# Attention with routed experts: x kept by rows in memory, leftover tokens fetched by an indirect read

## The chip, the cores and the metric

One core of one Trainium2 chip runs the whole program. The metric is device time of one execution in microseconds; the median of several runs counts. Engines: PE (TensorE, matmuls), DVE (VectorE), ACT (ScalarE), POOL (GpSimd), SP (SyncE, which here issues DMAs). Each works through its own instructions in order and waits for the others by semaphores.

## The reference

Attention over keys and values that are averaged in groups of 8 tokens, then a mixture of experts in which every token goes to the best expert (4) of its best group (4):

```
k_p, v_p = mean of k, v over groups of 8 tokens        # 8 batches, 8 heads, 576 tokens, 64
attn = softmax(q @ k_p.T / 8) @ v_p
x = attn.transpose(0, 2, 1, 3).reshape(4608, 512)
g_idx = argmax(x @ w_group); g_w = softmax of it at g_idx
e_idx = argmax(xg @ w_expert[g]); e_w = softmax of it at e_idx
out[token] = g_w * e_w * (relu(x @ w1[g, e]) @ w2[g, e])   # w1 512x1024, w2 1024x512, float32
```

## The kernel before

A batch is 576 tokens, in two halves of 288 (256 and 320 in batch 0). Attention of batch b+1 (class Att) is worked in between the pieces of the experts of batch b (class Moe). x stands transposed: features on partitions, 4 groups of 128, tokens along the free axis. For accuracy x and the weights are each split into a high part that PE reads fast and the low rest: x in tiles `xa`, `xb` (a half each, index 0 high, 1 low; from batch 3 on the unsplit x is in `xr`, L414), the weights by ACT's `cast` (L579, high) and `lo` (L585, `raw - high`, on POOL or DVE). `split` is the two together.

Almost all tokens of a batch want one and the same expert, the main one, which the kernel finds at run time. Moe does the whole batch with it: 16 `up` pieces (8 slices f of the hidden layer, two halves; 12 matmuls each, L602), after each of which ACT (L604) and `upd` on DVE (L610, L615) empty the PSUM tile `mm`, of which there are three; and 14 `down` pieces of 8 matmuls (L631, L642; in the last batch three of 16, L663), after which ACT scales and stores the rows (L636, L668, L683). A chunk of 64 rows is summed by DVE first (L675, `tail`); in batches 2 to 6 that happens one batch later, between the first `up` and its `upd`. The gate is zero for tokens of other experts.

Those are the leftovers. `count` (L483 to L485) counts a batch's tokens by expert; `keep_x` compares (L548 to L552), SP reads the answer, and writes the split x of the batch to memory (`xscr`, two DMAs, L555) only where there are leftovers. With these inputs batch 5 alone has some. In the last batch (class Left, `l.`) the generator `place` (`l.step`, L733 to L768) ranks all leftovers: two matmuls on `loh` with copies L734, masks L738 and L739, a scan and its like to L756, `pos`. `which` (L778 to L785) picks a batch and expert for a block of up to 32 tokens, `slots` (L793 to L810) makes a 128x32 one-hot matrix for each chunk of its tokens, `rows` (L816) turns these into row numbers. `fetch_x` (L834) reads that batch's x back, `whole` (L848) adds its parts, `turn` (L858, 20 PE transposes; copies L859) puts tokens on partitions, `gather` (L866, 40 matmul rows) picks the 32 wanted. `back` (L872), `up` (L880), `hback` (L887) and `down` (L896) work them through their expert, whose weights come by `fetch_a` (L838) and `fetch_b` (L843), and an indirect DMA of POOL scatters them into the output (L899). The later `fetch` calls and a loop at the end are for further blocks, of which there are none here.

What sets the order: the strings START, FIRST (batch 0), SECOND (1), STEADY (2 to 6) and LAST (7). Each name in them is a call, and every engine gets its instructions in the order of the calls: `m.` is the batch's experts, `a.`, `n.`, `x.`, `z.` the attention of this batch, of the next, and of those two and three further on, `w.` the next batch's experts, `p.` the previous one's. In attention, `sc` is scores, `mx`, `su_`, `nm` the softmax (L348, L368 to L370, L375), `pt` its transposition by DVE (L382), `av` the value product (L396), `avd` the emptying of its PSUM (L412, L414), `rt` the routing matmul (L425, L429), `xlo` the low part of x on POOL.

Of the kernel before, what the change touches and what calls it, by code (L numbers as in the profile page):

```python
# [47 lines left out]
m.down:0 w.load:1:2 m.down:1 w.load:1:3 n.sc:1 n.qb:2 n.mx:1 n.pt:0 n.sb:1 m.down:2 m.store:0 n.su_:1 n.nm:1:p x.load_v x.load_k m.down:3 w.split:1:0:p:2 m.down:4 n.sc:2 n.mx:2 n.pt:1 n.sb:2 w.split:1:1:p:2
# [952 lines left out]
```

## Time and profile before

| | us |
|---|---|
| median of 3 runs | 512.82 (512.74 to 513.46) |
| the profiled execution's own time | 513.9 |
| its span, first to last instruction | 512.2 |
| PE busy | 499.5 (98%) |
| DVE busy | 342.1 (67%) |
| POOL busy | 281.5 (55%) |
| ACT busy | 206.3 (40%) |

The granted TensorE clock was 0.995 of full. Busy time is the sum over an engine's instructions; the chain of work is followed back from the last instruction to what released each step. "Idle before, releaser" is how long an engine stood still ahead of an instruction and what ended that. A row of the timeline with xN is a run of N like instructions; the ends of PE rows are modelled and overlap the next row.

### The profile page before, as it was taken

The page shows a single profiled execution, that of the slowest core. Times are in us where ns is not written, and L with a number is a line of the kernel's source. Part 1 is how long each engine was busy: PE and PEld are TensorE (multiplying, and loading weights), DVE is VectorE, ACT ScalarE, POOL GpSimd, SP SyncE. Part 2 cuts the span into 40 slices and gives each one's busy share as a digit, 9 for nine tenths or more (in the row PEclk, how much of TensorE's full clock was granted, in tenths as well). Part 3 has the DMA queues.
Part 4 walks back from the last instruction along what each step waited for, and adds up shares of the span by engine and source line. Part 5 has one row for each costly group of instructions (what it writes and reads, how often), then busy time and mean ns, then how long its engine had stood idle before and what let it go on. Part 6 is the DMA issues. An engine that isn't in the chain of part 4 may idle for free.

```text
span 512.2 us, 14848 instructions
## 1 busy us (share of the span) xinstructions
PE 499.5 (98%) x6085; PEld 439.2 (86%) x6085; DVE 342.1 (67%) x900; ACT 206.3 (40%) x381; POOL 281.5 (55%) x242
## 2 busy tenths in 40 slices
PE   8899999999999999999999999999999999998996
PEld 6688986999789978899789978899789988898976
DVE  6876877678575869486775768476784763199602
ACT  2354324435217541455216551455324551444212
POOL 2386658455818595376728585476846471820400
PEclk9899999999999999999999999999999999999999
DMA  9699279995038976955197616985066100923741
GB/s 281 177 283 192 27 227 228 214 259 89 28 104 233 260 108 177 312 153 83 35 316 207 141 27 143 370 307 88 1 202 184 39 3 22 307 94 124 268 165 58
DMA packets 118110, 83.70 MB, mean 163 GB/s; under 512 B 71034, under 2 KB 93818, under 8 KB 117784
## 3 DMA queue, kind: packets, MB, share of 16 engines
q1 hardware_dynamic: 113408, 75.67, 55.1%
q10 hardware_dynamic: 4600, 7.02, 3.9%
q8 instruction: 49, 0.80, 0.7%
q14 instruction: 21, 0.17, 0.1%
q0 software_dynamic: 32, 0.04, 0.0%
HBM read 77.28 MB, written 28.53 MB: 207 GB/s over the span
## 4 chain that ended last, share of the span: by engine, by line
PE 90%; DVE 4%; DMA 1%; ACT 1%; issue 1%; POOL 1%; POOLq 0%; ACTq 0%
PE mm L602 36%; PE mm L631 30%; PE mm L642 5%; PE sc L336 5%; PE sc L396 4%; PE mm L947 2%; PE tp L429 1%; PE tp L425 1%; DMA out_dram<-y 1%; DMA out_dram<-q,idx 1%; DVE pT L382 1%; POOL p L375 1%; PE tp L299 1%; DVE p L357 1%; PE tp L462 1%
## 5 line engine op out<-in xcount | busy, mean ns | idle before, releaser
L631 PE MATMUL mm<-w,ht 128*128 128x512 f32 x744 | 172.0, 384 | 0.0
L585 POOL TENSOR_TENSOR w<-sw,w 128x1024 fp32r<-128x1024 f32 (+2 forms) x86 | 145.1, 1711 | 40.0 <-ACT w L579 39.9
L631 PEld LDWEIGHTS mm<-w,ht 128*128 128x128 f32 x744 | 137.0, 189 | 25.1 <-issue 6.7
L602 PE MATMUL mm<-xb,w 128*128 128x288 f32 (+1 forms) x768 | 106.7, 291 | 1.7 <-DVE ht L610 1.7
L602 PEld LDWEIGHTS mm<-xb,w 128*128 128x128 f32 x768 | 98.6, 189 | 5.5 <-ACT w L579 2.2
L602 PE MATMUL mm<-xa,w 128*128 128x288 f32 (+1 forms) x768 | 102.3, 286 | 0.5 <-ACT xa L401 0.5
L602 PEld LDWEIGHTS mm<-xa,w 128*128 128x128 f32 x768 | 97.1, 189 | 2.2 <-ACT xa L401 1.0
L604 ACT ACTIVATE ht<-mm 128x288 fp32r<-128x288 f32 (+2 forms) x128 | 52.5, 411 | 94.7 <-PE mm L602 93.0
L375 POOL TENSOR_TENSOR p<-p,su 128x864 f32<-128x864 f32 (+2 forms) x26 | 39.6, 1523 | 76.5 <-DVE su L370 72.0
L579 ACT CAST w<-sw 128x1024 fp32r<-128x1024 f32 x64 | 66.6, 1041 | 31.5 <-DMA sw<-in_moe_w_dram 29.2
L615 DVE SCALAR_TENSOR_TENSOR ht<-mm,ht 128x64 fp32r<-128x64 f32 (+4 forms) x192 | 37.1, 249 | 25.1 <-ACT ht L604 25.0
L636 ACT ACTIVATE y<-mm,gm 128x512 f32<-128x512 f32 x31 | 21.2, 685 | 61.2 <-PE mm L631 61.2
L610 DVE SCALAR_TENSOR_TENSOR ht<-mm,ht 128x288 fp32r<-128x288 f32 (+1 forms) x64 | 27.4, 430 | 13.8 <-ACT ht L604 13.8
L368 DVE TENSOR_REDUCE s<-p 128x12 f32<-128x864 f32 (+2 forms) x26 | 25.4, 976 | 16.5 <-ACT p L362 16.5
L362 ACT ACTIVATE p<-p 128x864 f32<-128x864 f32 (+2 forms) x26 | 22.6, 869 | 28.9 <-DVE p L357 23.6
L382 DVE STREAM_TRANSPOSE pT<-p 128x960 f32<-128x960 f32 (+2 forms) x26 | 28.5, 1095 | 6.7 <-POOL p L375 6.0
L642 PE MATMUL mm<-w,ht 128*128 128x512 f32 x128 | 29.4, 381 | 0.0
L396 PE MATMUL sc<-pT,v 32*64 32x288 f32 (+2 forms) x384 | 27.2, 413 | 1.1 <-DVE pT L382 1.1
L336 PE MATMUL sc<-kT,qT 64*32 64x72 f32 x2176 | 27.9, 230 | 0.2 <-issue 0.2
L336 PEld LDWEIGHTS sc<-kT,qT 64*32 64x32 f32 x2176 | 23.6, 105 | 5.2 <-issue 2.9
L675 DVE TENSOR_TENSOR y<-mm,y 64x512 f32<-64x512 f32 x8 | 5.5, 681 | 32.7 <-ACT y L647 21.7
L396 PE MATMUL tp<-pT,v 32*64 32x288 f32 (+2 forms) x384 | 27.2, 413 | 0.0
(227 smaller groups left out, 565.6 us busy)
## 6 DMA issues: line engine op xcount, KB each, us to landing
sw<-in_moe_w_dram SPq DMA_DIRECT2D x72, 512.0 KB
vv<-in_v_dram SPq DMA_DIRECT2D x27, 320.0 KB
q<-in_q_dram SPq DMA_DIRECT2D x112, 72.0 KB
xscr<-xa SPq DMA_DIRECT2D x7, 1152.0 KB
xscr<-xb SPq DMA_DIRECT2D x7, 1152.0 KB
kv<-in_k_dram SPq DMA_DIRECT2D x14, 512.0 KB
out_dram<-y ACTq DMA_DIRECT2D x23, 256.0 KB
pT<-xscr SPq DMA_DIRECT2D x2, 1152.0 KB
```

The costliest lines, as they stand in the source:

```text
L336: nc.tensor.matmul(ps[x][32 * g:32 * g + 32, SP * t:SP * t + SP], lhsT=s.qT[c][64 * x:64 * x + 64, g, 32 * t:32 * t + 32], rhs=s.kT[64 * x ...
L375: (nc.vector if eng == "v" else nc.gpsimd).tensor_tensor(out=p, in0=p, in1=bc(s.su[c][:, 0:w], SP), op=ALU.mult)
L382: nc.vector.transpose(out=s.pT[:, :, o:o + n].rearrange("p j (t i) -> p t j i", i=32), in_=probs[:, z:z + n // 32].rearrange("p t (j i) -> ...
L396: nc.tensor.matmul(banks[a][64 * x:64 * x + 64, 0:n], lhsT=s.v6[32 * a:32 * a + 32, 5 if x and i == 0 else j, :], rhs=s.pT[32 * a:32 * a + ...
L579: nc.scalar.copy(out=s.w[m, j][0], in_=raw)
L585: (nc.vector if eng == "v" else nc.gpsimd).tensor_tensor(out=wl[:, i:i + n], in0=s.raw[m, j][:, i:i + n], in1=wh[:, i:i + n].bitcast(F32), ...
L602: nc.tensor.matmul(ps[:, 0:n], lhsT=l[:, kc, fs], rhs=apart(s.a.xt[hf][:, r, kc]), start=(kc == 0 and i == 0), stop=(kc == 3 and i == 2))
L604: nc.scalar.activation(out=halves(ht[:, sl]), in_=joined(ps[:, 0:n]), func=AF.Relu)
L610: stt(out=halves(ht[:, 640:640 + n]), in0=ps, scalar=0.0, in1=halves(ht[:, 0:n].bitcast(F32)), op0=ALU.max, op1=ALU.subtract)
L615: stt(out=ht[:, at:at + hi - lo], in0=ps[:, a, lo:hi], scalar=0.0, in1=ht[:, t + lo:t + hi].bitcast(F32), op0=ALU.max, op1=ALU.subtract)
L631: nc.tensor.matmul(ps, lhsT=s.ht[f][:, 640 * l + o:640 * l + o + 128], rhs=apart(s.w[2, f // 2][r][:, f % 2, :]), start=(i == 0), stop=(i ...
L642: nc.tensor.matmul(ps, lhsT=s.ht[f][:, 512:640], rhs=apart(s.w[2, f // 2][r][:, f % 2, :]), start=(i == 0), stop=(i == 15))
```

## The change

x of every batch is kept, unsplit, in memory in row order: one row of 512 for each token (`xrow`). To that end `xr` becomes a tile of 18 blocks of 32 tokens, in each the 4 feature groups side by side, so that DVE can transpose 32x32 squares in place (`xt_`, six instructions of 128x384 for a batch) and four DMAs of SP write it, 288 KB each, without condition (`keep_x`). For batches 0 to 2, whose x was never kept unsplit, ACT writes `xr` from PSUM (`raw`), or POOL adds the two parts (`rawp`, first half of batch 0). Batch 0's `xr` goes out untransposed to `xraw` (`keep_raw`), is read back in batch 5 into the buffer of the values, `vv` (`again`), and is transposed and written by rows in batch 6. The comparison and SP's read of its answer go.

A new plan PENULT serves batch 6: `place` runs there up to the rank, and the first two `lo` of the next weights are on DVE there. In LAST, `which` and `slots` come early, `rows` stands between `up` pieces and gives a third column, the row numbers to read; `get` is an indirect DMA of POOL that reads the 32 wanted pieces straight into `xg`, four partitions of 128 features for each token. `xtiles`, `fetch_x`, `whole`, `turn` and `gather` are gone; `fetch_a` reads its weights with the features in another order, 16 DMAs in place of 4. `l.up` and `l.down` are one `down` piece earlier or more. In FIRST, `count` goes (in SECOND too) and `w.split:1:1` moves behind `n.su_:2 n.nm:2`.

```diff
-m.up:5:0 a.pt:4 n.vr:0 m.upd:5:0 m.up:6:0 m.upd:6:0 m.up:7:0 a.av:1 n.vr:1 n.vm a.rt:0 m.upd:7:0 a.avd:1 n.kr:0
+m.up:5:0 a.pt:4 n.vr:0 m.upd:5:0 m.up:6:0 m.upd:6:0 m.up:7:0 a.av:1 n.vr:1 n.vm a.rawp:0 a.rt:0 m.upd:7:0 a.avd:1 a.raw:1 n.kr:0
...
-m.down:5 m.store:1 m.down:6 n.su_:2 n.nm:2:p m.down:7 n.av:0 n.avd:0 x.load_qb:0 m.down:8 m.store:2 x.vr:0 w.load:2:0 w.load:2:1 n.pt:2 m.down:9 x.kr:0 n.av:1 n.rt:0 n.avd:1 m.down:10 x.kr:1 x.vr:1 x.vm x.load_qb:1 x.load_qb:2 x.load_qb:3 n.rt:1 m.down:11 m.store:3 n.route_g n.route_e:p m.down:12 n.gates n.gm_:p m.down:13 m.store:4
+m.down:5 m.store:1 m.down:6 n.su_:2 n.nm:2:p w.split:1:1:p:2 m.down:7 n.av:0 n.avd:0 n.raw:0 x.load_qb:0 m.down:8 m.store:2 x.vr:0 w.load:2:0 w.load:2:1 n.pt:2 m.down:9 x.kr:0 n.av:1 n.rt:0 n.avd:1 n.raw:1 m.down:10 x.kr:1 x.vr:1 x.vm x.load_qb:1 x.load_qb:2 x.load_qb:3 n.rt:1 m.down:11 m.store:3 n.route_g n.route_e:p m.down:12 n.gates n.gm_:p m.down:13 m.store:4
...
-x.qb:0 n.gates n.gm_ n.xlo:1 n.keep_x m.down:6 x.kt m.down:7 x.sc:0 x.mx:0 x.sd:0 w.cast:1:0 w.lo:1:0 w.load:2:0 m.down:8 x.ex:0 x.qb:1 w.cast:1:1 w.load:2:1 m.down:9
-x.su_:0 x.nm:0:p w.lo:1:1 m.down:10 m.down:11 m.down:12 w.cast:1:2 m.down:13 w.cast:1:3
+x.qb:0 n.gates n.gm_ n.xlo:1 m.down:6 x.kt m.down:7 x.sc:0 x.mx:0 x.sd:0 w.cast:1:0 w.lo:1:0 w.load:2:0 m.down:8 x.ex:0 x.qb:1 w.cast:1:1 w.load:2:1 m.down:9
+x.su_:0 x.nm:0:p w.lo:1:1 n.xt_:0 n.xt_:1 n.xt_:2 m.down:10 m.down:11 n.xt_:3 n.xt_:4 n.xt_:5 n.keep_x m.down:12 w.cast:1:2 m.down:13 w.cast:1:3
...
+PENULT = """
...
+m.up:7:1 m.upd:7:1 n.av:1 n.rt:0 n.avd:1 o.xt_:0 o.xt_:1 o.xt_:2 o.xt_:3 o.xt_:4 o.xt_:5 o.keep_x
+m.down:0 n.rt:1 l.step m.down:1 n.route m.down:2 m.down:3 m.down:4 n.main_expert w.load:1:0 w.load:1:1 w.load:1:2 w.load:1:3 m.down:5
+n.gates n.gm_ n.xlo:1 m.down:6 m.down:7 l.step l.step w.cast:1:0 m.down:8 l.step l.step n.xt_:0 n.xt_:1 n.xt_:2 w.lo:1:0:v w.load:2:0 m.down:9 n.xt_:3 n.xt_:4 n.xt_:5 n.keep_x w.cast:1:1 l.step l.step l.step l.step w.lo:1:1:v w.load:2:1
+m.down:10 l.step l.step l.step m.down:11 l.step l.step l.step l.step l.step m.down:12 m.down:13
...
-l.whole:1 l.turn:1 l.turn:0 l.whole:2 m.lo:2:3:p m.down:2 m.down:3 l.turn:2 m.down:4 l.gather m.down:5 l.back m.down:6 l.up m.down:7 l.hback
-m.down:8 l.down l.fetch_x l.fetch_a l.fetch_b m.down:13 m.down:9 m.down:10 l.slots m.down:11
+m.up:0:0 p.tail m.upd:0:0 l.step m.up:0:1 m.upd:0:1 l.step l.which m.up:1:0 m.upd:1:0 m.up:1:1 m.upd:1:1 l.slots
+m.up:2:0 m.upd:2:0 m.cast:1:2 m.up:2:1 m.lo:1:2:v m.upd:2:1 m.load:2:2 m.up:3:0 m.upd:3:0 m.cast:1:3 m.lo:1:3 m.load:2:3 l.rows l.oh m.up:3:1 m.cast:2:0 m.upd:3:1 l.get m.lo:2:0 l.tiles l.fetch_b:1 m.up:4:0 m.upd:4:0 m.cast:2:1 m.up:4:1 m.upd:4:1 m.lo:2:1
+m.up:5:0 m.upd:5:0 m.up:5:1 m.cast:2:2 m.upd:5:1 m.lo:2:2:v m.up:6:0 m.upd:6:0 m.up:6:1 m.cast:2:3 m.upd:6:1 m.lo:2:3:v l.fetch_a:1 m.up:7:0 m.upd:7:0 l.next_ m.up:7:1 m.upd:7:1
+m.down:0 m.down:1 l.back m.down:12 m.down:2 m.down:3 m.down:4 m.down:5 l.up m.down:6 l.hback m.down:7 l.down
+m.down:8 l.fetch_a l.fetch_b m.down:13 m.down:9 m.down:10 l.slots m.down:11
...
-    xscr = dram.tile([B, 128, 2, 4, S], F32, name="xscr")
+    xraw = dram.tile([128, S // 32, NG, 32], F32, name="xraw")
+    xrow = dram.tile([B * S, DM], F32, name="xrow")
...
-                s.xr = xp.tile([128, NG, S], F32, name="xr")
+                s.xr = xp.tile([128, S // 32, NG, 32], F32, name="xr")
...
+        def rows_(s, h):
+            o, n = s.half[h]
+            return s.rawt()[:, o // 32:(o + n) // 32].rearrange("p j g c -> p g j c")
...
-                    ts(out=s.rawt()[:, g, o:o + n], in0=ps, scalar1=0.125, scalar2=None, op0=ALU.mult)
+                    ts(out=s.rows_(h)[:, g], in0=by32(ps), scalar1=0.125, scalar2=None, op0=ALU.mult)
...
+        def raw(s, h):
+            o, n = s.half[h]
+            for ps, g in s.ta[h]:
+                nc.scalar.mul(out=s.rows_(h)[:, g], in_=by32(ps), mul=0.125)
+        def rawp(s, h):
+            o, n = s.half[h]
+            for g in range(NG):
+                nc.gpsimd.tensor_tensor(out=s.rows_(h)[:, g], in0=by32(s.xt[h][:, 0, g].bitcast(F32)), in1=by32(s.xt[h][:, 1, g].bitcast(F32)), op=ALU.add)
+        def xt_(s, u):
+            z = s.xr[:, 3 * u:3 * u + 3].rearrange("p j g c -> p (j g c)")
+            nc.vector.transpose(out=z, in_=z)
+        def keep_raw(s):
+            nc.sync.dma_start(out=xraw, in_=s.xr)
+        def again(s):
+            s.xr = sk.tile([128, 5, 512], F32, name="vv").rearrange("p a x -> p (a x)")[:, 0:NG * S].rearrange("p (j g c) -> p j g c", g=NG, c=32)
+            nc.sync.dma_start(out=s.xr, in_=xraw)
         def keep_x(s):
-            t = sm.tile([128, NE], F32, name="cr")
-            tt(out=t, in0=s.cnt, in1=s.moh, op=ALU.mult)
-            n = sm.tile([128, 1], F32, name="cm")
-            red(out=n, in_=t, axis=AX.X, op=ALU.add)
-            s.lf = sm.tile([128, 1], I32, name="lf")
-            ts(out=s.lf, in0=n, scalar1=float(S), scalar2=None, op0=ALU.is_lt)
-            left = nc.sync.value_load(s.lf[0:1, 0:1], min_val=0, max_val=1)
-            for h, (o, n) in enumerate(s.half):
-                nc.sync.dma_start(out=xscr[s.b][:, :, :, o:o + n], in_=s.xt[h].bitcast(F32), cond=left, cond_hint=False)
+            to = xrow[S * s.b:S * s.b + S].rearrange("(j i) (a x) -> a i j x", i=32, a=4)
+            for a in range(4):
+                nc.sync.dma_start(out=to[a], in_=s.xr[32 * a:32 * a + 32].rearrange("p j g c -> p j (g c)"))
...
+        def oh(s):
+            ts(out=s.ix, in0=s.mps[:, 2:3], scalar1=s.quarter, scalar2=None, op0=ALU.add)
+            ts(out=s.idx[:, 1:2], in0=s.mps[:, 0:1], scalar1=s.quarter, scalar2=None, op0=ALU.add)
+            nc.vector.tensor_copy(out=s.gl[:, 1:2], in_=s.mps[:, 1:2])
+        def get(s):
+            nc.gpsimd.indirect_dma_start(out=s.xg, out_offset=None, in_=xrow.rearrange("n (d c) -> (n d) c", d=4),
+                                         in_offset=bass.IndirectOffsetOnAxis(ap=s.ix.bitcast(U32), axis=0), bounds_check=4 * B * S - 1, oob_is_err=False)
...
+                for k in range(4):
+                    nc.sync.dma_start(out=s.wa[j][32 * k:32 * k + 32],
+                                      in_=w1x[bass.ds(s.re, 1), k, :, :, 256 * j:256 * j + 256].rearrange("o c a f -> c (o a) f"),
...
-        def whole(s, c):
-            o, n = CH[c]
-            (nc.gpsimd if c % 2 else nc.vector).tensor_tensor(
-                out=s.xh[0][:, :, o:o + n], in0=s.xh[0][:, :, o:o + n], in1=s.xh[1][:, :, o:o + n], op=ALU.add)
...
-                nc.tensor.transpose(out=ps[0:n, 128 * g:128 * g + 128], in_=s.xh[0][:, g, o:o + n], identity=ident)
-            (nc.vector.tensor_copy if c % 2 else nc.scalar.copy)(out=s.xr[0:n, c, :], in_=ps[0:n])
...
-                    nc.tensor.matmul(ps[32 * g:32 * g + BS, 0:128], lhsT=s.sl[c][0:n, 0:BS], rhs=s.xr[0:n, c, 128 * g:128 * g + 128],
-                                     start=(c == 0), stop=(c == NC - 1))
-            nc.scalar.copy(out=s.xg, in_=ps[:, 0:128])
...
-            run(LAST if b == B - 1 else STEADY, b)
+            run(LAST if b == B - 1 else PENULT if b == B - 2 else STEADY, b)
```

On PE, from the end of the last batch's `up` pieces to the end; before (`ident,pT` are the transposes of `turn`, `xb,q` is `gather`):

```order
L816 MATMUL tp<-kT,q 128x2 x5
L858 MATMUL tp<-ident,pT 128x128 x4
L858 MATMUL tp<-ident,pT 64x128 x4
L642 MATMUL mm<-w,ht 128x512 x8
L858 MATMUL tp<-ident,pT 128x128 x8
L631 MATMUL mm<-w,ht 128x512 x16
L858 MATMUL tp<-ident,pT 128x128 x4
L631 MATMUL mm<-w,ht 128x512 x8
L866 MATMUL tp<-xb,q 32x128 x20
L631 MATMUL mm<-w,ht 128x512 x8
```

and of the change, from the first `down` pieces on (L884 is `back`, L892 `l.up`, L908 `l.down`):

```order
L665 MATMUL mm<-w,ht 128x512 x16
L884 MATMUL tp<-ident,q 128x128
L676 MATMUL mm<-w,ht 128x512 x8
L665 MATMUL mm<-w,ht 128x512 x32
L892 MATMUL tp<-sw,q 32x256 x16
L665 MATMUL mm<-w,ht 128x512 x8
L899 MATMUL tp<-ident,q 128x128 x2
L665 MATMUL mm<-w,ht 128x512 x8
L908 MATMUL tp<-kv,q 32x128 x16
L908 MATMUL tp<-vv,q 32x128 x16
```

The transposes and `gather` are gone; the row numbers' matmul (`kT,q`) is not in this piece any more, it stands between `up` pieces.

On DVE at the seam of two batches, before (`y<-mm,y` is L675, the sum of the 64-row chunk):

```order
L368 TENSOR_REDUCE s<-p 128x12
L369 TENSOR_REDUCE su<-s 128x12
L370 RECIPROCAL su<-su 128x12
L675 TENSOR_TENSOR y<-mm,y 64x512
L610 SCALAR_TENSOR_TENSOR ht<-mm,ht 128x288
L382 STREAM_TRANSPOSE pT<-p 128x6x5x32
```

and of the change, the same place:

```order
L381 TENSOR_REDUCE s<-p 128x12
L382 TENSOR_REDUCE su<-s 128x12
L383 RECIPROCAL su<-su 128x12
L576 STREAM_TRANSPOSE xr<-xr 128x384 x6
L709 TENSOR_TENSOR y<-mm,y 64x512
L644 SCALAR_TENSOR_TENSOR ht<-mm,ht 128x288
L395 STREAM_TRANSPOSE pT<-p 128x6x5x32
```

Six transposes of the next batch's x stand between the reciprocal and that sum.

On ACT at the end, before (the activation with `gl` is `l.down`'s, which the scatter of POOL follows; each DMA is a store):

```order
L882 ACTIVATE q<-tp 128x256
L636 ACTIVATE y<-mm,gm 128x512
L683 DMA out_dram<-y 128x512
L898 ACTIVATE q<-tp,gl 128x128
L647 COPY y<-mm 64x512
L676 ACTIVATE y<-y,gm 64x512
L667 ACTIVATE y<-mm,gm 128x256
```

and of the change:

```order
L894 ACTIVATE q<-tp 128x256
L910 ACTIVATE q<-tp,gl 128x128
L670 ACTIVATE y<-mm,gm 128x512
L717 DMA out_dram<-y 128x512
L681 COPY y<-mm 64x512
L710 ACTIVATE y<-y,gm 64x512
L701 ACTIVATE y<-mm,gm 128x256
```

`l.down` now comes ahead of the third chunk's store, which was ahead of it.

## Rows read from the trace of the kernel before

**Rows 1.** page, part 1 (busy us, share, xcount) and part 4 (the chain by engine)
```profile
PE 499.5 (98%) x6085; PEld 439.2 (86%) x6085; DVE 342.1 (67%) x900; ACT 206.3 (40%) x381; POOL 281.5 (55%) x242
...
PE 90%; DVE 4%; DMA 1%; ACT 1%; issue 1%; POOL 1%; POOLq 0%; ACTq 0%
```

**Rows 2.** PE's waits: line <- releaser: us in total, times, longest
```profile
PE mm L602 <- DVE ht L610: 1.7, 1, 1.7
...
PE sc L396 <- DVE pT L382: 1.1, 1, 1.1
```

**Rows 3.** chain that ended last, at the end: start us, us, what
```profile
478.38 1.09 PE tp L858 x8
479.47 1.73 PE mm L642 x8
481.19 0.87 PE tp L858 x8
...
485.52 0.44 PE tp L858 x4
...
487.69 1.36 PE tp L866 x40
...
499.31 2.04 DMA out_dram<-y
...
502.34 3.69 DMA out_dram<-q,idx
...
506.09 1.69 DMA out_dram<-y
```

**Rows 4.** PE in order of time: start, us, line, operation, count
```profile
99.59 0.34 PE L483 MATMUL tp<-oh,ones 128*128 128x80 f32 x2
...
337.24 1.63 PE L602 MATMUL mm<-xa,w 128*128 128x288 f32 x12
...
502.20 5.52 PE L663 MATMUL mm<-w,ht 128*128 128x256 f32 x48
```

**Rows 5.** chain that ended last, late in the first batch (POOL, ahead of L382)
```profile
81.27 1.29 POOL w L585
82.56 1.60 POOL p L375
```

**Rows 6.** DVE in order of time in the last batch, with the idle time before
```profile
448.18 0.68 DVE L675 TENSOR_TENSOR y<-mm,y 64x512 f32<-64x512 f32 x1 [10.98 <-DMA out_dram<-y]
...
449.94 2.69 DVE L585 TENSOR_TENSOR w<-sw,w 128x1024 fp32r<-128x1024 f32 x1
...
465.80 1.22 DVE L585 TENSOR_TENSOR w<-sw,w 128x1024 fp32r<-128x1024 f32 x1
```

**Rows 7.** DVE groups by line and shape: count | busy us, mean ns | idle before
```profile
L382 DVE STREAM_TRANSPOSE pT<-p 128x960 f32<-128x960 f32 x21 | 24.6, 1174 | 5.3 <-POOL p L375 4.5
...
L382 DVE STREAM_TRANSPOSE pT<-p 128x640 f32<-128x640 f32 x4 | 3.3, 827 | 0.6 <-POOL p L375 0.6
...
L734 DVE COPY kv<-tp 128x320 f32<-128x320 f32 x4 | 1.7, 474 | 0.0
...
L738 DVE TENSOR_TENSOR kv<-kv 128x128 f32<-128x128 f32 x4 | 1.1, 283 | 0.0
...
L382 DVE STREAM_TRANSPOSE pT<-p 128x320 f32<-128x320 f32 x1 | 0.5, 512 | 0.8 <-POOL p L375 0.8
```

**Rows 8.** DVE at the seam of batches 4 and 5, in order of time
```profile
330.24 0.23 DVE L370 RECIPROCAL su<-su 128x12 f32<-128x12 f32 x1
333.77 0.68 DVE L675 TENSOR_TENSOR y<-mm,y 64x512 f32<-64x512 f32 x1 [3.30 <-ACT y L647]
```

**Rows 9.** issues on SP's queue in order of time: start, us of issuing, xcount
```profile
324.96 3.94 SPq L555 DMA_DIRECT2D xscr<-xb  x1
329.40 10.23 SPq L573 DMA_DIRECT2D sw<-in_moe_w_dram  x4
...
494.69 1.35 SPq L838 DMA_DIRECT2D sw<-in_moe_w_dram  x4
```

More of the change, by code (lines that the diff above doesn't have):

```diff
@@ L48 @@
[L48 to L49 removed]
+m.lo:2:2:p:2 n.kt m.cast:2:3 m.up:5:1 m.upd:5:1 a.gm_:p a.keep_raw m.lo:2:3:p:2 m.up:6:1 w.load:1:0 w.load:1:1 m.upd:6:1 n.sc:0 n.mx:0 n.sb:0 n.qb:1 m.up:7:1 m.upd:7:1 n.su_:0 n.nm:0:p
@@ L56 @@
-x.sc:0 x.mx:0 x.sb:0 m.down:10 x.qb:1 m.down:11 m.store:3 w.split:1:1:p:2 w.load:2:1 x.su_:0 x.nm:0:p m.down:12 w.cast:1:2 m.down:13 m.store:4
+m.up:0:0 x.load_v x.load_k m.upd:0:0 n.qb:0 m.up:1:0 m.upd:1:0 m.split:1:2:p:2 m.load:2:2 n.kt m.up:0:1 m.upd:0:1 a.xt_:0 a.xt_:1 m.split:1:3:p:2 m.load:2:3 m.up:1:1 m.upd:1:1 a.xt_:2 a.xt_:3 n.sc:0 n.mx:0 m.up:2:0 m.upd:2:0 n.sd:0 n.ex:0 n.qb:1 m.up:2:1 m.upd:2:1 n.su_:0 n.nm:0:p m.split:2:0:p:2
+m.up:3:0 m.upd:3:0 a.xt_:4 a.xt_:5 a.keep_x m.up:3:1 m.upd:3:1 n.sc:1 n.pt:0 n.mx:1 m.up:4:0 m.upd:4:0 n.sd:1 n.ex:1 n.qb:2 m.up:4:1 m.upd:4:1 n.su_:1 n.nm:1:p m.split:2:1:p:2 m.up:5:0 m.upd:5:0 m.split:2:2:p:2 m.up:5:1 m.upd:5:1 n.sc:2 n.mx:2 n.pt:1
@@ new lines @@
+x.load_qb:0 x.load_qb:1 x.load_qb:2 x.load_qb:3 m.up:6:0 m.upd:6:0 n.sd:2 n.ex:2 m.up:7:0 m.upd:7:0 m.up:6:1 n.su_:2 n.nm:2:p m.upd:6:1 m.split:2:3:p:2 m.up:7:1 m.upd:7:1 n.av:0 n.avd:0 n.raw:0 m.down:0 n.pt:2 x.vr:0 m.down:1 x.vr:1 x.vm n.rt:0 m.down:2 m.store:0 n.av:1 n.avd:1 n.raw:1 x.kr:0 m.down:3
+m.down:4 n.rt:1 n.route_g n.route_e:p x.kr:1 m.down:5 m.store:1 m.down:6 x.qb:0 m.down:7 x.kt n.main_expert w.load:1:0 w.load:1:1 w.load:1:2 w.load:1:3 n.gates n.gm_ m.down:8 m.store:2 m.down:9 w.split:1:0:p:2 w.load:2:0
@@ L57 @@
+x.sc:0 x.mx:0 x.sb:0 m.down:10 x.qb:1 m.down:11 m.store:3 w.split:1:1:p:2 w.load:2:1 x.su_:0 x.nm:0:p n.xt_:0 n.xt_:1 n.xt_:2 m.down:12 n.xt_:3 n.xt_:4 n.xt_:5 n.keep_x w.cast:1:2 m.down:13 m.store:4
 """
@@ L70 @@
-m.up:2:0 m.cast:2:1 l.step m.upd:2:0 l.step m.up:2:1 l.step m.upd:2:1 l.step m.up:3:0 l.step l.step m.upd:3:0 m.up:3:1 l.step l.step m.upd:3:1
-m.up:5:0 l.step l.step l.step l.step m.upd:5:0 m.lo:1:3 m.cast:2:2 m.up:4:0 l.step l.step l.which m.lo:2:2:v m.upd:4:0 m.lo:2:1:v
-m.up:6:0 m.cast:2:0 m.upd:6:0 m.up:5:1 m.lo:2:0:v m.up:4:1 m.up:6:1 m.cast:2:3 l.fetch_x l.tiles m.upd:5:1 m.upd:4:1 m.upd:6:1 l.slots m.down:0 m.down:1 l.fetch_a:1
-m.up:7:0 l.fetch_b:1 m.upd:7:0 l.whole:4 l.whole:0 m.up:7:1 l.rows l.next_ l.whole:3 m.upd:7:1 l.turn:3 l.turn:4 m.down:12
@@ L428, in rt @@
             for a in range(4):
[L429 removed]
+                nc.tensor.matmul(ps[32 * a:32 * a + 32, 0:n], lhsT=wr[:, a, :], rhs=s.rows_(h)[:, a], start=True, stop=True)
             nc.scalar.copy(out=lt[:, o:o + n], in_=ps[:, 0:n])
@@ L911, in block @@
             s.rows()
-            for c in range(NC):
-                s.whole(c)
-                s.turn(c)
+            s.oh()
+            s.get()
             s.next_()
-            s.fetch_x()
-            s.gather()
             s.back()
```

70 lines of the change are left out of this document (27 added, 43 removed).

## The prediction

> **What bounds the kernel now.** I read the engine totals first, then the chain of work that ended last, then the list of what TensorE waited for. TensorE (PE) is busy 499.5 of 512.2 us, and 90% of the chain is PE work [rows 1]. So another engine's microsecond is worth something only where PE waits for it, and a PE instruction taken out is worth its own chain time. The list of PE's waits has two that a change of order can remove: 1.7 us in the last batch, where `up` waits for DVE to empty a PSUM tile (L602 for L610), and 1.1 us in the first batch, where the value product L396 waits for DVE's transposed probabilities (L382) [rows 2]. Nothing in the steady batches shows up there at all. The reader is to see that the 90% leaves little for hiding: a gain has to be PE instructions gone or one of these two waits gone, and a loss has to be a new wait of PE or a longer tail after it.
>
> **The change, part by part.** The sum is made against the profiled execution: span 512.2 us, its own time 513.9 us; the median of the runs is 512.82 us, 0.6 above the span. I apply the difference to the median.
>
> *PE work that goes.* The leftover block no longer turns x on PE. The 20 transposes of L858 stand in the chain as 1.09, 0.87 and 0.44 us, together 2.40, and the 40 matmul rows of L866 as 1.36 [rows 3]. All of it is in the last batch with PE as the chain, and nothing replaces it on PE: the 32 wanted rows come by an indirect read. That is -3.76 us. What could take it back is the block's first matmul (L872, `back`) waiting for the read. The nearest row is the indirect scatter, 3.69 us from start to landing [rows 3]; with about 1 us to issue, the read, called after `up` 3:1, has eight `up` pieces (1.63 us of rows each, overlapping a little [rows 4]) and two `down` (1.73 each [rows 3]) before it is used, some 15 us. Hidden. The counts of batches 0 and 1 go too: two matmuls each, 0.34 us of rows that overlap their neighbours [rows 4]; I take half of it for each, -0.3 us together.
>
> *The wait in the first batch.* Before it POOL splits a weight slice (`w.split:1:1`, L585, the last part 1.29 us) and only then normalises p (L375, 1.60), which DVE transposes [rows 5]. The change puts the split behind that normalisation, so p is ready about 1.3 us or more sooner, and the 1.1 us [rows 2] go. What is late next there: the route matmul of the second half, whose PSUM tiles ACT now also reads for `raw` copies; I charge 0.15. Net -0.95 us. Behind the moved split the weights are wanted in the next batch, many us later.
>
> *The wait in the last batch.* Before, DVE there carries the block's bookkeeping. The plan for batch 6 takes the steps up to the rank into a stretch in which DVE idles 10.98 us [rows 6]. Into that hole go: four copies L734 (4 x 0.47 = 1.9), eight mask operations like L738 (8 x 0.28 = 2.2) and eleven more up to L756, of 0.23 to 0.29 us like it (2.7) [rows 7]; the six transposes of batch 7's x; and two weight splits. A split took DVE 1.22 us, and 2.69 in another place [rows 6]. The transposes: 128x320 took 0.512, 128x640 0.827, 128x960 1.174 [rows 7], so a 128x384 is 0.512 + 64 x 0.00098 = 0.575 us by itself, and about 0.5 in a row; six are 3.0 to 3.45. The sum is 6.8 + 3.2 + 2.4 = 12.4, or 15.4 with the dear splits, less 0.5 for the dropped comparison. So the evacuation L675 at the seam starts 1 to 4 us later than at 448.18; it has some 2.8 us before PE wants its tile (below). Then DVE has in the last batch 6.8 us less bookkeeping and three splits where it had four, but the slot masks are wanted already after `up` 3:0, since the row numbers are now matmuls in the middle of the `up` pieces. By laying these in order I get small waits of 0.4 and 0.2 us and then little: 0.9 us of stall in place of 1.67, bounds 0 and 2.5. Net -0.75 us.
>
> By itself, on the splits: at 449.94 the DVE split takes 2.69 us, at 465.80 1.22 [rows 6]. The Trainium skill (GPSIMD Engine Reference, Specifications) says that POOL and VectorE share their SBUF interfaces and contend when DVE has two SBUF inputs, as a split has. By that rule the price depends on what POOL does beside; since batch 6 takes the POOL splits themselves away from that stretch, it speaks for the low price here, and only with other POOL work for 15.4 in place of 12.4, which would make the stall about 2 us.
>
> *What each batch gains to do.* x is kept for all batches, where before the copy is conditional and batch 5 alone was written. Each batch from 1 on gets six in-place transposes on DVE at the seam, ahead of L675, behind the reciprocal. There DVE idles 3.30 us before L675 at 333.77 [rows 8]; six at 0.5 to 0.575 fill that hole to within 0.2 us. L675 ends at 334.45, and the third `up` piece of the batch, which I take for the first to need its tile, starts at 337.24 [rows 4]: 2.8 us more. So they cost nothing; what is queued behind them on DVE (L675, L610, the next L382) moves 0.2 us. I charge 0.3 us over all batches for this and for the strided writes and reads of x in 32-element runs, bounds 0 and 1.5.
>
> *Transfers.* Four unconditional writes of 288 KB per batch, 1.18 MB; batch 0's goes out, comes back and goes out again. On SP's queue they stand before the loads of the next weights (`sw`). The one batch that shows such a write is batch 5, 3.94 us of issuing on SP for the second of its two halves of 1.15 MB, with the loads after it at 329.40 taking 10.23 us to issue [rows 9]; no PE wait comes of it [rows 2]. Half of that batch's bytes in every batch should do no more. The weight fetch of the leftover block is now 16 issues where it was 4; four took 1.35 us [rows 9], so 16 are 5.4 us, ahead of `up` by seven `down` pieces or 12 us. Hidden.
>
> A sentence by itself: the pieces are 512 bytes long, and the Trainium skill (DMA: Bandwidth & Descriptors, Specifications) puts the smallest transfer for full rate at 512 bytes, so by it the writes run at full rate, just; no row of before has this pattern.
>
> *The tail.* Now `down` 8 comes behind the block's last matmul, so its store, on ACT's queue, must wait for the scatter; before it was the other way. With T the end of L896: activation 0.4 and issue 1.0 (before, some 1.0 lies between the landing of the store at 499.31 + 2.04 and the scatter's start) and scatter 3.69 [rows 3] end at T + 5.1; ACT is held at the store until then, and then needs the issue, a copy, L675, an activation and half an activation, about 2.7 us at 0.68 for L675 [rows 8] and like sizes for the rest, so the first half store goes at about T + 7.8 and lands 1.69 to 2.04 later [rows 3], T + 9.5 to 9.9. PE ends after two pieces of 1.73 [rows 3] and the last 5.52 [rows 4], T + 9.0. Before, PE's end (502.20 + 5.52 [rows 4]) and the landing of the first half (506.09 + 1.69 [rows 3]) coincided at 507.7. So the tail grows by 0 to 0.9, more if the scatter is slower; I take 0.4, bounds 0 and 1.5.
>
> **Sum.** -2.40 - 1.36 - 0.3 - 0.95 - 0.75 + 0.3 + 0.4 = -5.06, or 512.82 - 5.1 = 507.7 us.
>
> **Rivals.**
> *DVE too late (B).* The hole takes 15.4 us or the steps wait for each other across PE; then L675 starts past its slack, each `up` tile comes late in turn, and the rows' matmul, which stands between `up` pieces, makes PE wait for slots. Stall 2.5 to 4 us in place of 1.67. For it: PE waits for DVE there already [rows 2], and its order is now tighter. Against: 11 us of hole. It gives 509.3 to 511.
> *Slower (C).* The transposes at the seam cost much more than their row. They work in place on 128x384, and every row of that operation here goes from one buffer to another. The price decides at (3.30 + 2.8) / 6 = 1.02 us each; at 1.17 (the 128x960 row [rows 7]) L675 is late by 0.9 us, and PE with it, in each of six batches, 5.4 us, and the hole of batch 6 overflows by 7 us with two sets of six in or near it, of which some 3 reach PE: +8.4, so 516, with 513 to 518 for prices around it. Against it: the rows of that operation grow evenly with their width.
> *Tail (D).* The scatter's chain is longer by a microsecond than its row, all of which is after PE's end: 508.7 to 510.
> *The change does not do what it says (E).* The writes or the read back hold up weight loads until `up` or `down` waits for a cast, 0.5 to 1 us in each of eight batches: 511.7 to 515.7. Against it stands batch 5.
>
> **How the numbers follow.** The forecast 0.62, with its own range from 506.0 (all stalls gone, no new cost: 512.82 - 2.40 - 1.36 - 1.67 - 1.1 - 0.3) to 509.3; B 0.17; C 0.09; D 0.06; E 0.06. About 0.2%, 1.0 us, is what a measurement of this kernel can tell from no change. Faster than 511.8: the forecast, B and D, less some tails, and a little of E, 0.84; within 0.2%: 0.06; slower: most of C and half of E, 0.10. The range of 8 in 10 goes from 505.5 (a term of the sum too small by half a microsecond) to 512.0 (the lower edge of E); what it leaves out is C, most of E and the edges.
>
> **What would show it.** Right: no PE rows of L858 and L866; neither wait in the list of PE's waits; the transposes at 0.5 to 0.6 us and L675 at the seam of a steady batch moved by less than a microsecond; in the last batch PE waits of under 1 us at `up` or at the rows' matmul; ACT's store of `down` 8 idle until the scatter lands. Wrong: a PE wait on `up` in every batch (C), a cast waiting for `sw` (E), a PE wait of several us between 447 and 470 (B), a last PE instruction well ahead of the last evacuation (D).

## The result and the profile after

The changed kernel takes 506.73 us (median of 4 runs, 506.02 to 507.20) where the kernel before takes 512.78 (4 runs): a ratio of 0.9882 with a 95% interval of 0.9863 to 0.9900, 6.05 us faster. The forecast was 5.06 us faster, 507.7, in a range of 505.5 to 512.0.

The page of the changed kernel: PE's busy time fell by 5.4 us against [rows 1], DVE's rose by 15, and 96% of the chain is now PE.

```profile
PE 494.1 (98%) x6021; PEld 435.9 (86%) x6021; DVE 357.2 (71%) x919; ACT 211.0 (42%) x394; POOL 277.8 (55%) x248
...
PE 96%; DMA 1%; ACT 1%; issue 0%; DVE 0%; SPq 0%; ACTq 0%
```

PE's waits in the changed kernel (line, releaser: us in total, times, longest). Both waits of [rows 2] are gone. Of the waits of half a microsecond and more that are left, all lie in the first 30 us but for the second row, which comes in batch 1 ("issue": the profile shows nothing that PE waited for).

```profile
PE mm L349 <- ACT qT L330: 1.5, 1, 1.5
...
PE sc L349 <- issue: 0.8, 1, 0.8
PE mm L636 <- ACT xa L414: 0.6, 1, 0.6
```

To see where the time went, I cut both spans at three PE rows: the first `up` of batch 1, the first `up` of batch 7, and the end of the last PE row.

| profiled execution, us | to batch 1 | batches 1 to 6 | last batch | after PE's end | span |
|---|---|---|---|---|---|
| before | 96.65 | 350.72 | 60.35 | 4.48 | 512.2 |
| after | 94.35 | 351.70 | 54.01 | 4.94 | 505.0 |
| difference | -2.30 | +0.98 | -6.34 | +0.46 | -7.2 |

The first column's -2.30 holds 1.35 us that the change did not make: PE reached its very first `up`, ahead of all that the change touches on PE, at 26.34 us in place of 27.69, and in after_again, the changed kernel once more, at 27.49 (last section). Without it the spans differ by 5.85 us, close to the medians' 6.05.

The last batch of the changed kernel, PE in order of time (start, us, line, count). There is no idle time in these rows: the 54.01 us are PE's work. The row numbers' matmul (L853) stands between `up` pieces, `back` (L884) follows the first two `down` pieces, and no transposes or `gather` come after it.

```profile
455.07 1.63 PE L636 MATMUL mm<-xa,w 128*128 128x288 f32 x12
456.54 1.26 PE L853 MATMUL tp<-kT,q 128*128 128x3 f32 x10
457.73 1.74 PE L636 MATMUL mm<-xb,w 128*128 128x288 f32 x12
...
471.07 3.62 PE L665 MATMUL mm<-w,ht 128*128 128x512 f32 x16
474.52 0.27 PE L884 MATMUL tp<-ident,q 128*128 128x128 f32 x1
...
494.54 5.52 PE L697 MATMUL mm<-w,ht 128*128 128x256 f32 x48
```

The -6.34 us there are 2.40 and 1.36 of L858 and L866, 1.67 of the wait for DVE, and 0.59 of the ranking's matmuls, which now are in batch 6 (they stand in the +0.98); 0.3 are left over.

DVE in batch 6 of the changed kernel, in order of time: the stretch that held 10.98 us of idle time in [rows 6] is full, with the ranking's copies, six transposes, two weight splits at 1.18 and 1.22 us, and the masks, and L709 (L675 before) ends at 448.81. The third `up`, which needs its tile, begins at 448.99, without a wait, the second of the two PE rows below.

```profile
437.47 0.89 DVE L775 COPY kv<-tp 128x320 f32<-128x320 f32 x2 [1.14 <-PE tp L774]
438.28 1.49 DVE L576 STREAM_TRANSPOSE xr<-xr 128x384 f32<-128x384 f32 x3
439.69 1.18 DVE L619 TENSOR_TENSOR w<-sw,w 128x1024 fp32r<-128x1024 f32 x1
440.79 1.49 DVE L576 STREAM_TRANSPOSE xr<-xr 128x384 f32<-128x384 f32 x3
...
444.16 1.22 DVE L619 TENSOR_TENSOR w<-sw,w 128x1024 fp32r<-128x1024 f32 x1
...
448.13 0.68 DVE L709 TENSOR_TENSOR y<-mm,y 64x512 f32<-64x512 f32 x1
```

```profile
446.05 1.63 PE L636 MATMUL mm<-xa,w 128*128 128x288 f32 x12
...
448.99 1.63 PE L636 MATMUL mm<-xa,w 128*128 128x288 f32 x12
```

DVE at the seam of [rows 8], after: six transposes take 2.81 us, 0.47 each in a row, and the sum still waits 0.89 us for ACT, as it waited 3.30 before.

```profile
328.02 0.23 DVE L383 RECIPROCAL su<-su 128x12 f32<-128x12 f32 x1
328.17 2.81 DVE L576 STREAM_TRANSPOSE xr<-xr 128x384 f32<-128x384 f32 x6
331.87 0.68 DVE L709 TENSOR_TENSOR y<-mm,y 64x512 f32<-64x512 f32 x1 [0.89 <-ACT y L681]
```

### The profile page after: what moved, and what is told of

The parts are those of the page before. It is cut to its first block, busy times and chain, and to the rows that moved or that the text cites. A ratio compares the mean times of both kernels' runs of the same rounds, so it can differ in the third digit from the quotient of the medians.

```text
span 505.0 us, 14775 instructions
## 1 busy us (share of the span) xinstructions
PE 494.1 (98%) x6021; PEld 435.9 (86%) x6021; DVE 357.2 (71%) x919; ACT 211.0 (42%) x394; POOL 277.8 (55%) x248
## 4 chain that ended last, share of the span: by engine, by line
PE 96%; DMA 1%; ACT 1%; issue 0%; DVE 0%; SPq 0%; ACTq 0%
PE mm L636 39%; PE mm L665 33%; PE mm L676 6%; PE sc L349 5%; PE sc L409 4%; PE mm L956 2%; PE tp L447 1%; PE tp L443 1%; PE mm L697 1%; DMA sw<-in_moe_w_dram 1%; PE tp L312 1%; PE tp L409 1%; PE tp L480 1%; PE tp L328 0%; PE tp L908 0%
## 5 line engine op out<-in xcount | busy, mean ns | idle before, releaser
L619 POOL TENSOR_TENSOR w<-sw,w 128x1024 fp32r<-128x1024 f32 (+2 forms) x85 | 142.9, 1704 | 55.9 <-ACT w L613 55.7
L665 PEld LDWEIGHTS mm<-w,ht 128*128 128x128 f32 x744 | 137.1, 189 | 24.9 <-issue 6.1
L361 DVE TENSOR_REDUCE mx<-sc 128x12 f32<-128x864 f32 (+2 forms) x24 | 23.7, 987 | 7.7 <-PE sc L349 7.7
L676 PEld LDWEIGHTS mm<-w,ht 128*128 128x128 f32 x128 | 24.0, 189 | 3.5
## 6 DMA issues: line engine op xcount, KB each, us to landing
sw<-in_moe_w_dram SPq DMA_DIRECT2D x64, 512.0 KB
kv<-in_k_dram SPq DMA_DIRECT2D x14, 512.0 KB
```

What stands on the lines that cost most here:

```text
L619: (nc.vector if eng == "v" else nc.gpsimd).tensor_tensor(out=wl[:, i:i + n], in0=s.raw[m, j][:, i:i + n], in1=wh[:, i:i + n].bitcast(F32), ...
L665: nc.tensor.matmul(ps, lhsT=s.ht[f][:, 640 * l + o:640 * l + o + 128], rhs=apart(s.w[2, f // 2][r][:, f % 2, :]), start=(i == 0), stop=(i ...
L676: nc.tensor.matmul(ps, lhsT=s.ht[f][:, 512:640], rhs=apart(s.w[2, f // 2][r][:, f % 2, :]), start=(i == 0), stop=(i == 15))
```

## Experiments

Eleven kernels were run, each beside the kernel before. Most are the changed kernel with one thing altered. The table cuts their profiled executions as above; "ratio" is to the kernel before, with its interval.

| kernel | median, us | ratio | to batch 1 | batches 1 to 6 | last batch | after PE's end |
|---|---|---|---|---|---|---|
| after_again | 507.17 | 0.9858 (0.9834 to 0.9881) | 95.17 | 351.93 | 54.01 | 4.89 |
| first_old | 507.83 | 0.9880 (0.9857 to 0.9902) | 96.62 | 351.43 | 54.00 | 4.95 |
| tail_old | 507.00 | 0.9864 (0.9842 to 0.9885) | 93.51 | 351.96 | 54.01 | 4.92 |
| read_alone | 512.30 | 0.9966 (0.9949 to 0.9983) | 94.96 | 351.40 | 60.78 | 3.86 |
| read_alone_2 | 508.29 | 0.9929 (0.9901 to 0.9956) | 95.27 | 351.26 | 56.59 | 3.88 |
| write_twice | 512.95 | 0.9994 (0.9978 to 1.0010) | 94.53 | 353.03 | 59.25 | 3.99 |
| write_behind | 518.31 | 1.0100 (1.0068 to 1.0132) | 95.50 | 353.72 | 62.97 | 3.91 |
| write_but_0 | 509.85 | 0.9942 (0.9923 to 0.9960) | 94.56 | 352.94 | 55.02 | 5.68 |
| seam_8 | 507.33 | 0.9893 (0.9879 to 0.9908) | 95.00 | 351.66 | 54.01 | 4.93 |
| seam_12 | 513.11 | 1.0005 (0.9981 to 1.0029) | 95.19 | 357.34 | 54.01 | 4.86 |
| seam_18 | 530.08 | 1.0318 (1.0303 to 1.0333) | 95.06 | 374.38 | 54.00 | 4.96 |

**The yardstick.**

> The changed kernel as it is, as the yardstick for the other runs of this set. Both theories: about 0.988 of the kernel before, some 506.7 us where before is 512.8.

507.17 us. The last batch has 54.01 us again.

**The first batch's order.**

```diff
-... n.pt:1 n.sb:2
-m.down:5 m.store:1 m.down:6 n.su_:2 n.nm:2:p w.split:1:1:p:2 m.down:7 ...
+... n.pt:1 n.sb:2 w.split:1:1:p:2
+m.down:5 m.store:1 m.down:6 n.su_:2 n.nm:2:p m.down:7 ...
```

> The changed kernel with one thing undone: in the first batch the weight split goes back ahead of the normalisation of p. Theory (PE is the chain, and that wait was worth its length less 0.15): 0.95 us slower than the changed kernel, about 507.7, with a wait of PE for the transposed p of about 1.1 us in its list of waits. Rival (the wait is taken up by another one behind it): 506.7, and no change.

PE's wait is back, in the list of waits:

```profile
PE sc L409 <- DVE pT L395: 1.2, 1, 1.2
```

I compare with after_again from the first `up` on (27.67 us here, 27.49 there), since the moved split cannot reach what lies ahead of it. To batch 1 it is 1.27 us longer, and batches 1 to 6 are 0.50 shorter, so 0.77 in the profiles; the medians differ by 0.66, with intervals that overlap. The 0.50 is in one wait of batch 1, in after_again and here:

```profile
PE sc L349 <- issue: 1.1, 1, 1.1
```

```profile
PE sc L349 <- issue: 0.6, 1, 0.6
```

So the theory stands with a size of 0.7 to 0.8 and not 0.95, and the rival is true in part: a wait behind takes up some of what the order gives.

**The indirect read alone.** Is the gain the PE work, or the order?

Batch 6 gets the steady plan without `o.again`, with `o.xt_` and `o.keep_x` behind `n.avd:1`; the last batch gets the plan of before without `xtiles`, `fetch_x`, `whole`, `turn` and `gather`, and with the read (one line of it, against the kernel before):

```diff
-... m.up:7:1 l.rows l.next_ l.whole:3 m.upd:7:1 l.turn:3 l.turn:4 m.down:12
+... m.up:7:1 l.rows l.oh l.get l.next_ m.upd:7:1 m.down:12
```

> The indirect read alone in place of fetch, add, transposes and gather; the ranking steps, the slots and the row numbers stay in the last batch where they were before, and batch 6 has the steady plan plus batch 0's six transposes. Theory: PE's 3.76 us, the first batch's 0.95 and the counts' 0.3 are kept, but PE's wait of 1.7 us for DVE in the last batch comes back: about 508.4. Rival (that wait went because DVE lost the additions and copies of the turn): no wait, 506.7. Rival (what gained was the order, not the PE work): 510 or more.

512.30 us, the third of the expected cases, and at first sight the PE work bought nothing: the last batch takes 60.78 us, before 60.35. PE in order of time shows the wait for DVE as it was, and a second one, for a weight split on POOL:

```profile
466.42 3.24 PE L638 MATMUL mm<-xb,w 128*128 128x288 f32 x24 [1.67 <-DVE ht L646]
...
482.18 8.21 PE L667 MATMUL mm<-w,ht 128*128 128x512 f32 x29 [2.24 <-POOL w L621]
```

POOL in order of time says why. The read (L864) stands ahead of that split in POOL's queue, and POOL stands still for 26.78 us until it can go; the split sits behind it. (The profile names L817, a step of DVE at 478.10; the row numbers `ix`, which the read needs, were written from 477.41 to 477.63.)

```profile
478.51 1.23 POOL L864 DMA_INDIRECT q<-xrow,ix  x1 [26.78 <-DVE kb L817]
479.78 2.35 POOL L621 TENSOR_TENSOR w<-sw,w 128x1024 fp32r<-128x1024 f32 x1
```

After the 2.24 us of waiting PE's granted clock was 0.61 from 482 to 486 (window table: us, busy times of PE, PEld, DVE, ACT and POOL, then clock, DMA share, GB/s), and the stretch cost 4.2 us in all (60.78 less the 56.59 of the next kernel), not 2.24.

```profile
482.00:486.00 4.00, 3.82 (x11) 3.06 (x12) 0.87 (x6) 0.69 (x1) 0.13 (x1) 0.61 0.64 144
```

**The same, with POOL's queue in another order.**

Against read_alone:

```diff
-... m.up:7:1 l.rows l.oh l.get l.next_ m.upd:7:1 m.down:12
-m.lo:2:3:p m.down:2 ...
+... m.up:7:1 m.lo:2:3:p l.rows l.oh l.get l.next_ m.upd:7:1 m.down:12
+m.down:2 ...
```

> As read_alone, but the last weight split on POOL (2:3) stands ahead of the indirect read on POOL's queue, not behind it. In read_alone PE waited 2.24 us for that split, which stood behind the read, and ran at a granted clock of 0.74 in the 6 us around. Theory (queue order on POOL made the new wait): that wait goes and with it about 1.7 us of half clock, so 508.4, with DVE's 1.67 us in the last batch still there. Rival (the read alone gains nothing because PE has nothing to do while weights are late): another wait of 2 us or more in its place, 511 to 512.

508.29 us, the theory's 508.4. (Three of its twelve executions took 512.4 to 514.0, at a mean granted clock of 0.993 to 0.995 where the others had 0.996 to 0.999. No trace of one of the three is kept, so what they lost is open.) The wait for POOL is gone, that for DVE is there:

```profile
466.60 3.24 PE L638 MATMUL mm<-xb,w 128*128 128x288 f32 x24 [1.68 <-DVE ht L646]
```

The last batch takes 56.59 us, 3.76 less than before: just the 2.40 + 1.36 of [rows 3]. And it takes 2.58 more than in the changed kernel, the 1.67 of the wait, the 0.59 of the ranking's matmuls and 0.3. So both parts of the last batch's gain are shown apart: PE's work by the read, the wait by the plans for batches 6 and 7. The read by itself can lose all of its gain to one instruction behind it on POOL.

**The tail.**

```diff
-... m.down:5 l.up m.down:6 l.hback m.down:7 l.down
-m.down:8 l.fetch_a l.fetch_b m.down:13 ...
+... m.down:5 l.up m.down:6 l.hback m.down:7 m.down:8
+l.down l.fetch_a l.fetch_b m.down:13 ...
```

> The changed kernel with the leftover block's second layer behind down 8 again, so that the third store is ahead of the scatter, as before. Theory (the tail is bound by PE's last piece, since the store was held 0.36 us and not until T + 5.1): within 0.3 us of the changed kernel. Rival (the prediction's tail term): 0.4 us faster, 506.3. Rival (the scatter becomes the end): 0.5 to 1 us slower.

507.00 us against 507.17; last batch and tail are alike to 0.03 us. The prediction's hold of the third store does not exist at its size. In the changed kernel ACT's rows show the store going out 0.36 us after its activation ends (L717 at 494.06), while the scatter of POOL started at 491.77; the forecast had it held until T + 5.1, which is 496.

```profile
491.12 0.37 ACT L910 ACTIVATE q<-tp,gl 128x128 f32<-128x128 f32 x1 [5.30 <-PE tp L908]
493.01 0.69 ACT L670 ACTIVATE y<-mm,gm 128x512 f32<-128x512 f32 x1 [1.53 <-PE mm L665]
494.06 0.34 ACTq L717 DMA_DIRECT2D out_dram<-y  x1
```

**Twice the bytes.**

```diff
-            to = xrow[S * s.b:S * s.b + S].rearrange("(j i) (a x) -> a i j x", i=32, a=4)
+            for x in (xrow, xrow2):
+                to = x[S * s.b:S * s.b + S].rearrange("(j i) (a x) -> a i j x", i=32, a=4)
...
```

> The changed kernel, but each batch's x is written by rows twice, to two places in memory: 1.18 MB and four SP issues more in each batch. Theory (the writes are hidden, and the loads behind them on SP have several us of cover): within 0.3 us of 506.7. Rival (the writes cost PE through late weight loads): 0.1 to 0.4 us in each of eight batches, 507.5 to 510.

512.95 us, all of the gain lost, and not in eight batches: 5.24 us in the last one and 1.25 in batch 3. On SP's queue the eight writes of batch 0's x take 11.26 us of issuing, ahead of the next weights' loads, which start at 438.72; in the changed kernel the four writes take 3.78 and the loads start at 432.12.

```profile
425.57 11.26 SPq L591 DMA_DIRECT2D xrow<-vv  x8
438.72 7.98 SPq L609 DMA_DIRECT2D sw<-in_moe_w_dram  x5
```

DVE, which now splits those weights in batch 6, waits for the cast, with the masks and the sum L711 behind it, and PE at the third `up` waits for the sum:

```profile
445.08 1.22 DVE L621 TENSOR_TENSOR w<-sw,w 128x1024 fp32r<-128x1024 f32 x1 [3.80 <-ACT w L615]
```

```profile
454.29 3.25 PE L638 MATMUL mm<-xa,w 128*128 128x288 f32 x12 [3.62 <-DVE y L711]
```

The 12 matmuls behind the wait take 3.25 us where they take 1.63 otherwise. 3.62 and 1.62 make the 5.24.

**The writes behind the loads.**

```diff
-... n.avd:1 o.xt_:0 o.xt_:1 o.xt_:2 o.xt_:3 o.xt_:4 o.xt_:5 o.keep_x
-... w.load:1:0 w.load:1:1 w.load:1:2 w.load:1:3 m.down:5
+... n.avd:1 o.xt_:0 o.xt_:1 o.xt_:2 o.xt_:3 o.xt_:4 o.xt_:5
+... w.load:1:0 w.load:1:1 w.load:1:2 w.load:1:3 o.keep_x m.down:5
```

> As write_twice, but in batch 6 the writes of batch 0's x stand behind the loads of the next weights on SP's queue, not ahead of them. In write_twice the loads were issued 6.6 us later, the cast 7.8 us later, and PE waited 3.62 us and then ran 12 matmuls in 3.25 us. Theory (what costs is the place on SP's queue in batch 6, not the bytes): the last batch is back at 54 us and the whole at 508 (with the 1.25 us that the third batch lost). Rival (the bytes themselves are too many): 511 or more, and PE still waits for DVE there.

518.31 us: the theory misses, and the rival's case (511 or more, PE waiting for DVE) comes about, but from another cause. The first split on DVE no longer waits, but then DVE stands 6.52 us ahead of L788, the first ranking step that writes into `vv`:

```profile
455.91 0.23 DVE L788 TENSOR_SCALAR vv<-kv 128x128 f32<-128x128 f32 x1 [6.52 <-DMA sw<-in_moe_w_dram]
```

The transfer named there writes `sw`, which that instruction does not use; it writes the buffer out of which batch 0's x is copied, and that copy had been put later. I read the wait as one for the copy, and the times of the packets bear this out: the eight writes are 4608 packets of 512 bytes, the last of them ends at 455.29, and L788 starts 0.62 us later. PE waits 7.2 us in the end. So the run does not part the bytes from the place on SP's queue.

**All but batch 0's twice.**

```diff
-            for x in (xrow, xrow2):
+            for x in (xrow, xrow2)[:2 if s.b else 1]:
```

> As write_twice, but batch 0's x (written in batch 6, ahead of the loads of the last batch's weights) is written once; the other seven are written twice. Theory (PE's 3.62 us and the slow matmuls behind them came from that one write standing before the loads on SP's queue): the last batch is back at 54 us and the whole at about 508.5, the 1.25 us of the third batch staying. Rival (the bytes of batch 7's doubled write, or of all, make the loads late): PE waits for DVE again at the last seam, 511 to 513.

509.85 us, between the two: 1.3 above the theory and 1.2 below the rival. The last batch is at 55.02 us: the wait of 3.62 is gone, and two small ones are left, 0.54 and 0.17. Batch 3's 1.3 us stay. With the single write the loads go out at 433.56:

```profile
425.51 3.79 SPq L591 DMA_DIRECT2D xrow<-vv  x4
433.56 9.17 SPq L609 DMA_DIRECT2D sw<-in_moe_w_dram  x5
```

So 4.2 of the 5.2 us in write_twice's last batch came from one write's place ahead of the loads; the other seven doubled cost 2.3 us together in the two batches (1.3 and 1.0) and, in this run, 0.7 more after PE's end, whose cause I did not look for.

**How full the seam is.** Blocks are turned three times, which leaves the data as one turn does; at four seams (the x of batches 3 to 6). The diff is seam_12's; seam_8 has `u < 1`, seam_18 `u < 6`.

```diff
-            nc.vector.transpose(out=z, in_=z)
+            for i in range(3 if 3 <= s.b <= 6 and u < 3 else 1):
+                nc.vector.transpose(out=z, in_=z)
```

> The changed kernel with 12 transposes in place of 6 at four seams (batches 3 to 6; half of the blocks are turned three times, which leaves the same data). 12 x 0.468 = 5.6 us, against a gap of 2.81 + 0.89 = 3.70 us of transposes and idle and 2.8 us of slack behind it. Theory (gap and slack hide them): within 0.3 us of 506.7. Rival (there is no slack behind the gap): 1.9 us at each seam, 514.

> The same with 18 transposes at four seams (every block three times): 8.4 us. Theory (gap 3.70, slack 2.8, the rest falls on PE): 1.9 us at each of four seams, about 514.4, with a wait of PE for DVE at up. Rival (the slack is larger, or DVE catches up in later gaps): under 2 us in all. Rival (no slack): 4.7 us at each, 525.

> Eight transposes at four seams in place of six (one block turned three times). With 12 the transposes took 6.50 us, L675's sum was late by 1.07 us for the third up and a later score waited 0.79 more; so the direct wait begins at 5.4 us of transposes, and eight take some 4.1. Theory (gap and slack hide up to 5.4 us): within 0.3 us of the changed kernel, no wait of PE for DVE. Rival (the loss begins where the idle gap of 3.7 us ends): 0.4 us at each seam, 1.6 in all.

seam_8: 507.33 us, no PE wait for DVE; the eight take 4.04 us, beyond the idle gap of 3.7 at no cost. seam_12: 513.11, and 1.6 to 2.2 us at each of three seams (none at that into batch 6). The theory misses, and the rival's 514 comes about without its reason: with no slack behind the gap, 6.50 us would have cost 2.8 at each. For the twelve took 6.50 us, not 5.6. A repeated turn of a block took 0.61 us where a first one took 0.47: (6.50 less 2.81) / 6 here, and in seam_18 (10.17 less 2.81) / 12.

At the seam into batch 4:

```profile
273.95 6.50 DVE L577 STREAM_TRANSPOSE xr<-xr 128x384 f32<-128x384 f32 x12
280.37 0.65 DVE L710 TENSOR_TENSOR y<-mm,y 64x512 f32<-64x512 f32 x1
```

PE waits at the third `up`, and once more, for a transposed q that DVE brings late because of it:

```profile
281.07 1.74 PE L637 MATMUL mm<-xa,w 128*128 128x288 f32 x12 [1.07 <-DVE y L710]
...
289.48 0.74 PE L349 MATMUL sc<-kT,qT 64*32 64x72 f32 x50 [0.79 <-DVE qT L335]
```

6.50 less 1.07 is 5.4 us: up to there this seam hides transposes, about 0.9 us for each of six. It is the tightest. Into batch 3 the wait at `up` is 0.74, into batch 5, where the gap of 3.70 and the slack of 2.8 were read, there is none in the list, and half of the 1.6 us lost is the later wait of the scores. The seams are not alike: in the changed kernel the transposes begin 2.90, 1.34, 2.88 and 4.87 us ahead of the first `up` of batches 3 to 6.

seam_18: 530.08, 15.7 above the theory and 5 above the rival without slack; 18 took 10.17 us, the wait at `up` into batch 4 is 4.67, 3.6 more than in seam_12 for 3.67 more of transposes. The theory lacked two things. The transposes were dearer and the cover was less than it had them: the four waits at `up` (4.41, 4.67, 4.02, 1.48) make 14.6 us in place of 7.6. And the clock: 0.50 in the 5 us behind the wait, where the same 12 matmuls take 3.25 us.

```profile
289.77 3.25 PE L637 MATMUL mm<-xa,w 128*128 128x288 f32 x12 [4.67 <-DVE y L710]
```

```profile
289.00:294.00 5.00, 4.23 (x17) 4.23 (x18) 4.96 (x10) 1.89 (x4) 0.00 (x0) 0.50 0.74 142
```

## Why the prediction was right, step by step

*PE work removed, -3.76.* read_alone_2 measures the same 3.76. Its cover, the read done long before use, held: the read went at 460.70 and `back` used it at 474.52, without a wait.

*First batch, -0.95 and counts, -0.3.* Too large together: forecast -1.25, measured -0.55. Without the start's 1.35 the stretch to batch 1 is 0.95 shorter with batch 0's count in it, so the 0.15 that I charged for the next wait was rather 0.3. The count of batch 1 went as well, but batch 1 became 0.40 us longer: the "issue" row of PE's waits, 0.84 us, was 0.23 before. (after_again has -1.28 and +0.62, so -0.66, and 1.06 in that row.) The forecast looked for the next wait among the route matmuls; it stood in the next batch's scores, and first_old shows it take up 0.50 of what the order gives. What PE waits for there the profile doesn't show, and I leave it open.

*Last batch's wait, -0.75.* The term that was mis-sized: 0.9 us were to be left of the 1.67, none were. The hole of batch 6 took what I laid into it at the low price: the splits at 1.18 and 1.22 us, the transposes at 0.47 to 0.5, so that L709 started 2.1 us after the first `up`, where L675 had started 0.8 after it. That was just enough: at this seam no scores stand between the first `up` pieces, the third begins 2.94 us after the first and not 4.28 as in a steady batch, so the slack was some 1.45 us and not the 2.8 that I used, and 0.18 were left of it. The small waits that I got from laying DVE's work in order by hand (0.4 and 0.2 us, and margins on them) did not come. That is 0.9 us more than forecast. With the seam's 0.3, which did not come, and 0.3 in the last batch that I cannot assign it outweighs the 0.7 that the first two batches fell short, so part of the total's closeness is luck.

*The price of the splits.* At 449.94 of before POOL worked on a split of its own and DVE's took 2.69 us; in batch 6 of the changed kernel POOL has none, and both took 1.2. read_alone has the last batch's plan of before and so POOL's split back beside DVE's, and there DVE's took 2.69 again, POOL's row first:

```profile
448.17 2.37 POOL L621 TENSOR_TENSOR w<-sw,w 128x1024 fp32r<-128x1024 f32 x1 [3.33 <-ACT w L615]
```

```profile
448.93 2.69 DVE L621 TENSOR_TENSOR w<-sw,w 128x1024 fp32r<-128x1024 f32 x1
```

The Trainium skill's rule (GPSIMD Engine Reference, Specifications) on the shared SBUF interfaces agrees with these rows.

*The seam, +0.3.* Batches 2 to 5 are the same to 0.01 us. The price of 0.5 to 0.575 was right (0.47 in a row). The slack of 2.8 us behind the gap holds where it was read, at the seam into batch 5: seam_12 has no wait at `up` in the list there. The seam into batch 4 has less, and begins to pay at 5.4 us. Rival C's point, 1.02 us each, is nearer to 0.9 there, and is paid for twice, by `up` and by the next scores.

*Transfers.* Hidden, as forecast, but my evidence was thin: I had argued from batch 5, and the place that matters was batch 6, where the writes of two batches, the loads of the next weights and DVE's splits follow each other. There one more write of 1.18 MB ahead of the loads costs 4 to 5 us (write_twice, write_but_0). Rival E was closer than the 0.06 that I gave it.

*The tail, +0.4.* The number came out, 0.46 us more after PE's end, by no merit of the step: tail_old has the old order and the same tail, and the third store went 0.36 us after its activation. From the end of the last store's issue to the end of the span it was 3.58 us before, 4.03 in the changed kernel and 2.96 in read_alone_2; what sets that is open.
